# A state-space layer and a dilated attention in one kernel: loads, a matrix's layout and small work moved

## The chip, the cores and the metric

The kernel runs on one core of one Trainium2 chip. The metric is the device time of one execution in microseconds (us), and of several executions the median. The engines are TensorE (PE, matmuls; PEld is its weight loads), VectorE (DVE), ScalarE (ACT), GpSimd (POOL) and SyncE (SP), which issues most of the DMAs.

## The reference

Two layers on two inputs x of 2048 x 448 each, put side by side in the output:

```
A:  Lam_bar = exp(exp(log_dt) * (Lambda_re + i Lambda_im))
    B_bar   = ((Lam_bar - 1) / Lam) * (B_re + i B_im)
    h[t]    = Lam_bar * h[t-1] + B_bar x[t]            (448 complex states, t = 0..2047)
    y[t]    = 2 * Re(C h[t]) + x[t] * Dskip
B:  q, k, v = x @ wqkv  (16 heads of 28)
    logits over the 8 positions s, s-2, ..., s-14; softmax; sum of v; @ wo
```

## The kernel before

**Part B** turns x so that features lie on partitions. The first 512 rows are loaded plainly (`xn`, two DMAs on SP) and turned by PE (`turn_x`, L196, four times four transpositions into PSUM, then a copy by DVE or ACT); the rest comes by transposing DMAs. k's and q's projections (`proj_t`, L253) and v's (`proj`, L239) follow. The logits are products of q with shifted k on DVE (`products`, L298, in six groups of q and k channels, each 1.67 us) summed over channels by PE (`sums`, L315). The softmax (`softmax`, L344) turns the logits back with PE, takes maxima on DVE, subtracts them on PE and exponentiates on ACT. `pv` (L400) is a long line of DVE multiplications and additions; its result is turned by a DMA (`tail`, L422), multiplied by wo on PE (`out`, L432), copied out of PSUM and stored. The last of the four wo steps, `wo[3]`, copies by turns on ACT and DVE (L440).

**Part A** works in real pairs of states, seven blocks m of 64 states, and in time chunks of 16 with four sub-steps b. `params` (L528) computes powers of Lam_bar on DVE and ACT from `prow`, three rows of parameters turned by PE (`turn_params`, L523). `mat` (L596) makes from each power a block matrix on DVE by one broadcast multiplication with `Dm`; B's factor has the key "g" and a layout of its own. Level 1 (`level1_halves`, `level1`) applies B and the powers within a chunk; `scan` (L666) runs seven doubling steps over chunks; `ends` (L689) gives the carried state G; `correct` (L706) adds power times G to each state, either on PE with an identity matmul and a copy by ACT ("A"), or by one matmul and an addition on DVE ("V"); `y` (L722) multiplies by C and adds the skip term by matmuls with `Dg`, four diagonal matrices that `skip` (L580) makes on ACT from `drow`.

**What sets the order.** `lanes` (L97) issues matmuls of half height two at a time, one per half of the array, in numbered steps s; a group must be done on one half before the other half continues it, with a tiny memset on POOL (`spot`) between. `weave` is a list of (step, functions): at that step the functions' work is issued. BEGIN (L46) holds the steps of `first`, `second` and `third`, which start DVE's products and matrices; WEAVE those of the sums; 168 to 211 those of the softmax; 242 that of `skip`. After `lanes`, the remaining level 1, scans, ends and wo steps are issued in program order, and the tail's PE order is written by hand in `line`, with a "V" correction's matmul put in every 1.55 us (L881). `each` (L861) places a correction behind every DVE operation of the last `pv` from the ninth on. `cx.warm` issues matmuls on zeros at the start. Loads on SP run in program order; ACT's queue has three: log_dt's row and the two DMAs of k's weights.

Of the kernel before, what the change touches and what calls it, by code (L numbers as in the profile page):

```python
# [15 lines left out]
bf16 = mybir.dt.bfloat16  # L16

S = 2048
D = 448
T = 16  # L20
NCH = 128
KT = 4
KP = 112
KA = 128
# [10 lines left out]
NM = 7  # L35
MP = 8
PL = 64
# [8 lines left out]
BEGIN = [26, 45, 67]  # L46
# [114 lines left out]
class PartB:  # L161
# [55 lines left out]
    def load_w(self, src, dst, n, eng):  # L217
        v, r = self.B_wqkv[:, src:src + n], (KT - 1) * KA
        eng.dma_start(self.wn[:, 0:KT - 1, dst:dst + n], v[0:r].rearrange("(k p) c -> p k c", p=KA))
        eng.dma_start(self.wn[:, KT - 1, dst:dst + n], v[D - KA:D])  # L220

    def load_wo(self):
        nc = self.nc
        wo = self.wo_p
        wo_v = self.B_wo.rearrange("(h d) c -> h d c", h=H)
        for dl in range(8):
            nc.sync.dma_start(wo[dl * H:(dl + 1) * H, 0, 0:KT - dl // 4], wo_v[:, dl::8])
        nc.sync.dma_start(wo[PL:KA, 1], wo[0:PL, 0])
        nc.sync.dma_start(wo[0:PL, 1, 1:KT], wo[PL:KA, 0, 0:KT - 1])
# [192 lines left out]
    def tail(self, hf, jl0, acc, last):  # L422
        nc, pool, cx = self.nc, self.pool, self.cx
        if self.oT is None:
            self.oT = pool.tile([KA, 2, 14, NCH], bf16, name="oT", tag="bX")
        oT, flat = self.oT[:, self.oi % 2], acc.rearrange("p j d h -> p (j d h)")
        self.oi += 1
        n = 7 if last else 14
        for c in range(0, 14, n):
            nc.sync.dma_start_transpose(oT[:, c:c + n], flat[:, c * KA:(c + n) * KA])  # L430

        def out(i):  # L432
            done = []
            for odd in range(2):
                ps = cx.ps([NCH, D], f32, "wo_ps", "lg")
                for k in range(KT):
                    done.append(nc.tensor.matmul(ps[:], lhsT=oT[:, 7 * i + 3 * odd + k, :], rhs=self.wo_p[:, odd, k, :],  # L437
                                                 start=(k == 0), stop=(k == KT - 1)).ins)
                yb = cx.ya[:, 4 + 2 * i + odd] if last else pool.tile([NCH, D], bf16, name="yb", tag="yb", bufs=4)[:]
                cx.ev("V" if last and odd else "A", yb, ps[:])  # L440
                nc.sync.dma_start(self.out_b[:, hf * HJ + jl0 + 2 * i + odd, :], yb)
            return done

        return out if last else lambda: [out(i) for i in range(2)]


class PartA:
# [25 lines left out]
    def load_params(self):  # L473
        nc, pool = self.nc, self.pool
        self.prow = pool.tile([3 * NM, 2, PL], bf16, name="prow")
        self.drow = pool.tile([KT, KA], bf16, name="drow")
        for i, src in enumerate((self.A_logdt, self.A_Lre, self.A_Lim)):
            v = src.rearrange("(m p) -> m p", p=PL).unsqueeze(1).to_broadcast([NM, 2, PL])
            (nc.scalar, nc.sync, nc.sync)[i].dma_start(self.prow[i * NM:(i + 1) * NM], v)

    def load_d(self):
        nc = self.nc
# [33 lines left out]
    def load_x(self):  # L516
        self.xT = self.pool.tile([KA, 4, KT, NF], bf16, name="xaT", tag="xin")
        xv = self.A_x[0].rearrange("(n b) d -> n b d", b=4)
        for b in range(4):
            self.nc.sync.dma_start_transpose(self.xT[:, b, 0:KT - 1, :], xv[:, b, 0:(KT - 1) * KA])  # L520
            self.nc.sync.dma_start_transpose(self.xT[:, b, KT - 1:KT, :], xv[:, b, D - KA:D])

    def turn_params(self):  # L523
        self.pt = self.cx.ps([NCH, 3 * NM], bf16, "pt_p", "mm")
        self.cx.chain(self.nc.tensor.transpose(self.pt[:], self.prow[:].rearrange("m r p -> m (r p)"),
                                               self.cx.ident[0:3 * NM, 0:3 * NM]).ins)
# [67 lines left out]
            self.cx.order(self.mat(key, self.Scat[:, NPW if i == "g" else i]), after, "NoSync")  # L594

    def mat(self, key, scal):  # L596
        if key == "g":
            sh = [NCH, NM, 2, PL]
            t_ = self.pool.tile(sh, bf16, name="matg")
            in0 = self.Dm[:, :, 0].unsqueeze(1).unsqueeze(1).to_broadcast(sh)  # L600
            in1 = scal[:, :, 0:NM].rearrange("p h m -> p m h").unsqueeze(3).to_broadcast(sh)
            self.mats[key] = t_[:].rearrange("p m h q -> p m (h q)")
        else:
            sh = [NCH, 2, PL, MP]
            t_ = self.pool.tile(sh, bf16, name=f"mat{key}")
            in0, in1 = self.Dm[:].unsqueeze(1).to_broadcast(sh), scal.unsqueeze(2).to_broadcast(sh)
            self.mats[key] = t_[:].rearrange("p h q m -> p m (h q)")
        return self.nc.vector.tensor_tensor(t_[:], in0, in1, op=ALU.mult).ins

    def setup_c(self, *ms):  # L610
# [129 lines left out]
def body(ctx: ExitStack, tc: tile.TileContext, A_x, A_Lre, A_Lim, A_Bre, A_Bim, A_Cre, A_Cim, A_logdt, A_Dskip,  # L740
         B_x, B_wqkv, B_wo, out):
    nc = tc.nc
# [7 lines left out]
    b.alloc()  # L750
    b.load_xn(0, 2)
    a.load_params()
    b.load_w(D, 0, D, nc.scalar)
    b.load_xn(2, 4)
    cx.consts()
    a.consts()
# [11 lines left out]
    b.zero_halo(b.vd)  # L768
    b.load_wo()
    a.load_c()  # L770
    cx.warm(8)
    a.turn_params()
    turns = [lambda i=i: b.turn_x(i, "VAVV"[i], ("pt", "lg")[i // 2]) for i in range(4)]
    for f in turns[:2]:
        for ins in f():
            cx.chain(ins)
    a.params(b.turned["V"])
    cx.warm(2)

# [4 lines left out]
    def early(*keys):  # L784
        for k in keys:
            ins = a.mat("g" if k == "g" else KPOW[k], a.Scat[:, NPW if k == "g" else k])
            if b.product is not None:
                cx.order(ins, b.product, "NoSync")
            b.product = ins

    def first():
        early(0)
        b.products(0, 0)
        return ()

    def second():
        b.products(0, 0, (2,), (2,))
        early(3)
        return ()

    def third():
        b.products(0, 1, (0, 1))
        early("g", 4)
        return ()

    values = [b.proj(j, "A") for j in (*range(HJ, T), 6, 7, 4, 5, 2, 3, 0, 1)]
    qk, soft = b.qk(), {}
    weave = [(5, turns[2:] + [later]), (BEGIN[0], [first]), (BEGIN[1], [second]), (BEGIN[2], [third])]
    weave += [(s_, [f]) for s_, f in zip(WEAVE, qk)]
    weave.sort(key=lambda x: x[0])  # L810

# [24 lines left out]
        return next(soft["pv"]) + next(soft["pv"])  # L836

    weave += [(168, [turn])] + [(171 + 2 * i, [lambda i=i: soft[1][0][2 + i]()]) for i in range(2)] + [(177, [prepare])]
    weave += [(181, [begin]), (199, [more]), (211, [more])]
    weave += [(242, [a.skip])]  # L840
    cx.lanes([b.proj_t(t0, t1, g, "A") for t0, t1, gs in ((0, 256, (0, 1, 2, 4, 5, 6)), (256, 512, (0, 1, 2)), (0, 512, (3,)), (256, 512, (4, 5, 6)))
              for g in gs]
             + [b.proj_t(*t, g, "A") for t in parts for g in range(7)] + values
             + [a.level1_halves(b_, m) for b_ in range(4) for m in range(*MH[0])], weave, 20)
    at0, put, wo = soft[0][1], soft["put"], b.outs
    deque(soft["pv"], 0)
    deque(b.pv(1, soft[1][1], 4, 8, between=[put(11, 12), put(), put(1, 2)]), 0)
    a.alloc_scan()
    for mh in range(3):
        if mh:  # L850
# [5 lines left out]
        a.ends(mh)  # L856
    cx.ya = pool.tile([NCH, 8, D], bf16, name="ya", tag="cn")
    line, extra, steps = [], [], []
    todo = [(b_, m) for b_ in range(3) for m in range(NM)][5:]

    def each(ins):  # L861
        cx.vchain(ins)
        steps.append(ins)
        if len(steps) >= 9 and todo:
            extra.extend(a.correct(*todo.pop(0), "V"))

    def wo_line(lists):
        return [(i, 0.19) for l_ in lists for i in l_]

    for m in range(5):  # L870
        line += a.correct(0, m, "A")
    line += wo_line(wo[1]())
    deque(b.pv(0, at0, 0, 4, each=each), 0)
    deque(b.pv(0, at0, 4, 8, True, each=each), 0)
    for b_, r in itertools.product((3, 0, 1, 2), range(4)):
        line += a.y(r, b_)
# [41 lines left out]
```

## Time and profile before

| what | us |
|---|---|
| median of 3 runs (143.95, 144.22, 144.97) | 144.22 |
| the profiled execution | 144.79 |
| its span, first to last instruction | 142.7 |
| PE busy | 135.9 |
| DVE busy | 125.5 |
| ACT busy | 88.0 |
| PE's first matmul at | 1.25 |
| DVE's last pv operation ends at | 132.10 |

The profile is one execution. Times in it are from the span's start. A row of the timeline gives start, duration, engine, line, operation and shapes, and in brackets how long the engine had been idle and what ended that. Rows of several instructions in a pipeline last longer than their number times the distance of two: three matrices take 1.89 us, so 0.61 each, where one alone takes 0.67 to 0.69.

### The profile page before, as it was taken

The page shows a single profiled execution, that of the slowest core. Times are in us where ns is not written, and L with a number is a line of the kernel's source. Part 1 is how long each engine was busy: PE and PEld are TensorE (multiplying, and loading weights), DVE is VectorE, ACT ScalarE, POOL GpSimd, SP SyncE. Part 2 cuts the span into 40 slices and gives each one's busy share as a digit, 9 for nine tenths or more (in the row PEclk, how much of TensorE's full clock was granted, in tenths as well). Part 3 has the DMA queues.
Part 4 walks back from the last instruction along what each step waited for, and adds up shares of the span by engine and source line. Part 5 has one row for each costly group of instructions (what it writes and reads, how often), then busy time and mean ns, then how long its engine had stood idle before and what let it go on. Part 6 is the DMA issues. An engine that isn't in the chain of part 4 may idle for free.

```text
span 142.7 us, 3299 instructions
## 1 busy us (share of the span) xinstructions
PE 135.9 (95%) x1259; PEld 77.9 (55%) x1263; DVE 125.5 (88%) x157; ACT 88.0 (62%) x193; POOL 10.6 (7%) x108
## 2 busy tenths in 40 slices
PE   6999999999999999999969999999999999999991
PEld 2466445444566654356645655569555655555540
DVE  4499989989999889999999999999799999999011
ACT  3476678667686653845599976899862322345440
POOL 7311100101010001001120000000000000000000
PEclk9999999999999999999999999999999999999999
DMA  4979899999964869990042000082012731112963
GB/s 107 303 155 158 185 228 114 195 194 158 176 117 97 179 102 259 253 218 8 0 82 47 5 0 0 10 183 71 0 67 96 158 103 64 64 64 96 138 214 103
DMA packets 45166, 17.03 MB, mean 119 GB/s; under 512 B 37267, under 2 KB 44769, under 8 KB 45151
## 3 DMA queue, kind: packets, MB, share of 16 engines
q1 hardware_dynamic: 44586, 16.36, 55.9%
q10 hardware_dynamic: 565, 0.46, 1.1%
q8 instruction: 10, 0.16, 0.6%
q14 instruction: 5, 0.04, 0.1%
HBM read 3.91 MB, written 3.67 MB: 53 GB/s over the span
## 4 chain that ended last, share of the span: by engine, by line
PE 78%; DVE 9%; ACT 9%; issue 2%; POOL 0%; ACTq 0%; DVEq 0%; POOLq 0%
PE qk_ps L130 16%; PE y_ps L731 15%; PE l1h L130 7%; PE l L639 7%; PE wo_ps L437 6%; PE v_ps L130 5%; PE lg L323 5%; PE co L711 3%; PE warm L73 3%; ACT G L703 2%; DVE pr L312 2%; PE y_ps L727 2%; PE l L684 2%; ACT pbuf L687 2%; DVE pvb L414 1%
## 5 line engine op out<-in xcount | busy, mean ns | idle before, releaser
L414 DVE TENSOR_TENSOR pvb<-attn,vd 128x1792 bf16<-128x1792 bf16 (+1 forms) x33 | 34.3, 1055 | 0.0
L417 DVE TENSOR_TENSOR pvb<-pvb 128x1792 bf16<-128x1792 bf16 (+1 forms) x29 | 30.5, 1051 | 0.3
L130 PE MATMUL qk_ps<-xbT,wqkv_nat 64*128 64x512 bf16 (+1 forms) x210 | 24.0, 335 | 0.4 <-POOL spot L139 0.3
L312 DVE TENSOR_TENSOR pr<-q,kd 128x3072 bf16<-128x3072 bf16 x11 | 19.0, 1753 | 1.0 <-ACT q L156 0.6
L734 ACT CAST ya<-y_ps 128x448 bf16<-128x448 f32 x16 | 8.5, 532 | 18.5 <-PE y_ps L731 18.5
L731 PE MATMUL y_ps<-Ccat,h 128*128 128x448 bf16 x84 | 18.7, 352 | 0.0
L130 PEld LDWEIGHTS <-wqkv_nat 64*128 64x128 bf16 x210 | 11.0, 94 | 10.8 <-POOL spot L139 3.1
L130 PE MATMUL l1h<-xaT,Bcat 64*128 64x512 bf16 x112 | 15.6, 377 | 0.0
L437 PE MATMUL wo_ps<-wo_p,oT 128*128 128x448 bf16 x64 | 14.1, 352 | 0.0
L156 ACT CAST kd<-qk_ps 128x512 bf16<-128x512 f32 (+4 forms) x26 | 10.4, 423 | 4.5 <-PE qk_ps L130 4.3
L130 PE MATMUL v_ps<-wqkv_nat,xbT 64*128 64x448 bf16 x112 | 13.1, 361 | 0.0
L639 PE MATMUL l<-xaT,Bcat 128*128 128x512 bf16 x45 | 12.6, 379 | 0.1
L715 DVE TENSOR_TENSOR h<-co,h 128x512 bf16<-128x512 f32 x16 | 10.9, 683 | 0.8 <-PE co L711 0.7
L156 ACT CAST q<-qk_ps 128x512 bf16<-128x512 f32 (+2 forms) x23 | 9.9, 455 | 2.0 <-PE qk_ps L130 1.9
L731 PEld LDWEIGHTS <-h 128*128 128x128 bf16 x84 | 7.6, 98 | 5.6
L130 PEld LDWEIGHTS <-Bcat 64*128 64x128 bf16 x112 | 7.1, 94 | 5.5 <-issue 0.8
L139 POOL MEMSET spot<- 1x1 f32 x63 | 5.6, 89 | 59.3 <-PE qk_ps L130 25.8
L156 ACT CAST vd<-v_ps 128x448 bf16<-128x448 f32 x16 | 7.6, 528 | 3.7 <-PE v_ps L130 3.5
L650 ACT CAST h<-l1h 128x512 bf16<-128x512 f32 x12 | 6.4, 592 | 5.7 <-PE l1h L130 5.7
L130 PEld LDWEIGHTS <-xbT 64*128 64x128 bf16 x112 | 7.3, 145 | 4.1 <-issue 1.3
L687 ACT CAST pbuf<-l 128x512 bf16<-128x512 f32 (+2 forms) x21 | 8.9, 425 | 1.0 <-PE l L684 0.8
L312 DVE TENSOR_TENSOR kd<-q,kd 128x3072 bf16<-128x3072 bf16 x5 | 8.8, 1755 | 0.7 <-ACT q L156 0.7
(133 smaller groups left out, 212.7 us busy)
## 6 DMA issues: line engine op xcount, KB each, us to landing
out_dram<-ya SPq DMA_DIRECT2D x20, 112.0 KB, 1.7
out_dram<-yb SPq DMA_DIRECT2D x12, 112.0 KB, 1.8
vd<-vd SPq DMA_DIRECT2D x1, 784.0 KB, 5.4
wqkv_nat<-in_B_wqkv_dram SPq DMA_DIRECT2D x2, 336.0 KB
vd<-vd SPq DMA_DIRECT2D x1, 588.0 KB
xn<-in_B_x_dram SPq DMA_DIRECT2D x2, 224.0 KB, 3.9
cn<-in_A_C_re_dram SPq DMA_DIRECT2D x4, 98.0 KB, 3.2
cn<-in_A_C_im_dram SPq DMA_DIRECT2D x4, 98.0 KB, 3.4
```

Source lines behind the costliest of these rows:

```text
L130: ins = mm(g["ps"], lhsT=l_, rhs=r_, start=first, stop=not (g["left"][0] or g["left"][1]), skip_group_check=True).ins
L156: return self.nc.scalar.copy(out, in_).ins
L312: self.queued(V.tensor_tensor(pr, q[0][:, qu].unsqueeze(2).to_broadcast([KA, KT - 1, 4, n]), self.shifted(self.kT[:, 2 * i + qu], s), op=A ...
L323: out.append(mm(lg[32 * t:32 * t + 32, n * qu:n * qu + n], lhsT=l_, rhs=r_, start=not (s or qu or c), stop=(s == 1 and c == KT - 1), skip_ ...
L414: each(V.tensor_tensor(t_[:, c0:c1], at[:, w, jl0 + c0:jl0 + c1, :].unsqueeze(2).to_broadcast([NCH, c1 - c0, DH, H]), self.vd[:, off + c0: ...
L417: ins = V.tensor_tensor(acc[:, c0:c1], acc[:, c0:c1], t_[:, c0:c1], op=ALU.add).ins
L437: done.append(nc.tensor.matmul(ps[:], lhsT=oT[:, 7 * i + 3 * odd + k, :], rhs=self.wo_p[:, odd, k, :], start=(k == 0), stop=(k == KT - 1)) ...
L639: nc.tensor.matmul(ps[:], lhsT=self.Bcat[:, m, k, :], rhs=self.xT[:, b, k, :], start=(k == 0), stop=(b == 0 and k == KT - 1))
L687: nc.scalar.copy(dst[:, :, PAD:], ps[:])
L715: cx.vchain(nc.vector.tensor_tensor(h, ps[:], h, op=ALU.add).ins)
L731: out.append(nc.tensor.matmul(ps[:], lhsT=self.state(m, r, b), rhs=self.C[:, m, :], start=False, stop=(m == NM - 1), skip_group_check=True ...
L734: nc.scalar.copy(ya, ps[:])
```

## The change

- k's weights: four row blocks in two DMAs, blocks 0 and 1 on SP, 2 and 3 on ACT's queue, where it was blocks 0 to 2 and then 3, both on ACT's. Lambda_im's row goes to ACT's queue, ahead of the weights; SP issues its half of the weights in that row's place, ahead of the second half of x.
- Seven warm-up matmuls instead of eight at the start; the first turn of x precedes the turn of the parameters; the third and fourth turn of x come at step 8 instead of 5.
- B's factor matrix is made in the layout of the other matrices (one form for all).
- DVE's order: matrix 1 comes after the third step's edge products, matrix 4 between the two next products, and the two last scan matrices right after "g" and 8, where they were made in the second `pv`.
- The softmax's `more` of step 199 comes at 201; `skip` at 206 instead of 242.
- Three corrections by ACT instead of five, eighteen by DVE instead of sixteen, beginning one `pv` operation later.
- The last `wo` step: three copies by ACT, the fourth halved between ACT and DVE.

```diff
+    def load_wk(self):
+
+        v = self.B_wqkv[:, D:2 * D]
+        self.nc.sync.dma_start(self.wn[:, 0:2, 0:D], v[0:2 * KA].rearrange("(k p) c -> p k c", p=KA))
+        v = v[2 * KA:3 * KA].unsqueeze(1)
+        v = bass.AP(v.tensor, v.offset, [list(v.ap[0]), [v.ap[0][0] * (D - 3 * KA), 2], list(v.ap[2])])
+        self.nc.scalar.dma_start(self.wn[:, 2:KT, 0:D], v)
...
-                cx.ev("V" if last and odd else "A", yb, ps[:])
+                half = D // 2 if last and i and odd else D
+                cx.ev("A", yb[:, 0:half], ps[:, 0:half])
+                if half < D:
+                    cx.ev("V", yb[:, half:], ps[:, half:])
...
-            (nc.scalar, nc.sync, nc.sync)[i].dma_start(self.prow[i * NM:(i + 1) * NM], v)
+            (nc.scalar, nc.sync, nc.scalar)[i].dma_start(self.prow[i * NM:(i + 1) * NM], v)
...
+    pt = None
+
     def turn_params(self):
+        if self.pt is not None:
+            return
...
     def mat(self, key, scal):
-        if key == "g":
-            sh = [NCH, NM, 2, PL]
-            t_ = self.pool.tile(sh, bf16, name="matg")
-            in0 = self.Dm[:, :, 0].unsqueeze(1).unsqueeze(1).to_broadcast(sh)
-            in1 = scal[:, :, 0:NM].rearrange("p h m -> p m h").unsqueeze(3).to_broadcast(sh)
-            self.mats[key] = t_[:].rearrange("p m h q -> p m (h q)")
-        else:
-            sh = [NCH, 2, PL, MP]
...
+        sh = [NCH, 2, PL, MP]
+        t_ = self.pool.tile(sh, bf16, name=f"mat{key}")
+        in0, in1 = self.Dm[:].unsqueeze(1).to_broadcast(sh), scal.unsqueeze(2).to_broadcast(sh)
+        self.mats[key] = t_[:].rearrange("p h q m -> p m (h q)")
...
-    b.load_w(D, 0, D, nc.scalar)
+    b.load_wk()
...
-    cx.warm(8)
-    a.turn_params()
+    cx.warm(7)
...
     for f in turns[:2]:
         for ins in f():
             cx.chain(ins)
+        a.turn_params()
...
     def first():
-        early(0)
         b.products(0, 0)
...
     def second():
         b.products(0, 0, (2,), (2,))
-        early(3)
+        early(0)
...
     def third():
-        b.products(0, 1, (0, 1))
-        early("g", 4)
+        b.products(0, 1, (0,))
+        early(3)
+        b.products(0, 1, (1,))
+        early("g", 4, 11, 12)
...
-    weave = [(5, turns[2:] + [later]), (BEGIN[0], [first]), (BEGIN[1], [second]), (BEGIN[2], [third])]
+    weave = [(8, turns[2:] + [later]), (BEGIN[0], [first]), (BEGIN[1], [second]), (BEGIN[2], [third])]
...
-    weave += [(181, [begin]), (199, [more]), (211, [more])]
-    weave += [(242, [a.skip])]
+    weave += [(181, [begin]), (201, [more]), (211, [more])]
+    weave += [(206, [a.skip])]
...
-    deque(b.pv(1, soft[1][1], 4, 8, between=[put(11, 12), put(), put(1, 2)]), 0)
+    deque(b.pv(1, soft[1][1], 4, 8, between=[put(), put(), put(1, 2)]), 0)
...
-    todo = [(b_, m) for b_ in range(3) for m in range(NM)][5:]
+    todo = [(b_, m) for b_ in range(3) for m in range(NM)][3:]
...
-        if len(steps) >= 9 and todo:
+        if len(steps) >= 10 and todo:
...
-    for m in range(5):
+    for m in range(3):
         line += a.correct(0, m, "A")
```

In the built program, PE has three matmuls fewer, DVE the same products and pv operations in the same order, and SP and ACT's queue as many DMAs as before; the lanes' own order of matmuls is unchanged but for what is woven in. On SP one store of `wo[2]` now stands ahead of the first of the last two transpositions instead of behind it.

More of the change, by code (lines that the diff above doesn't have):

```diff
@@ L596, in mat @@
     def mat(self, key, scal):
-        if key == "g":
-            sh = [NCH, NM, 2, PL]
-            t_ = self.pool.tile(sh, bf16, name="matg")
-            in0 = self.Dm[:, :, 0].unsqueeze(1).unsqueeze(1).to_broadcast(sh)
-            in1 = scal[:, :, 0:NM].rearrange("p h m -> p m h").unsqueeze(3).to_broadcast(sh)
-            self.mats[key] = t_[:].rearrange("p m h q -> p m (h q)")
-        else:
-            sh = [NCH, 2, PL, MP]
-            t_ = self.pool.tile(sh, bf16, name=f"mat{key}")
-            in0, in1 = self.Dm[:].unsqueeze(1).to_broadcast(sh), scal.unsqueeze(2).to_broadcast(sh)
-            self.mats[key] = t_[:].rearrange("p h q m -> p m (h q)")
+        sh = [NCH, 2, PL, MP]
+        t_ = self.pool.tile(sh, bf16, name=f"mat{key}")
+        in0, in1 = self.Dm[:].unsqueeze(1).to_broadcast(sh), scal.unsqueeze(2).to_broadcast(sh)
+        self.mats[key] = t_[:].rearrange("p h q m -> p m (h q)")
         return self.nc.vector.tensor_tensor(t_[:], in0, in1, op=ALU.mult).ins
@@ L838, in body @@
     weave += [(168, [turn])] + [(171 + 2 * i, [lambda i=i: soft[1][0][2 + i]()]) for i in range(2)] + [(177, [prepare])]
-    weave += [(181, [begin]), (199, [more]), (211, [more])]
-    weave += [(242, [a.skip])]
+    weave += [(181, [begin]), (201, [more]), (211, [more])]
+    weave += [(206, [a.skip])]
+    weave.sort(key=lambda x: x[0])
     cx.lanes([b.proj_t(t0, t1, g, "A") for t0, t1, gs in ((0, 256, (0, 1, 2, 4, 5, 6)), (256, 512, (0, 1, 2)), (0, 512, (3,)), (256, 512, (4, 5, 6)))
```

## The prediction

> **What bounds the kernel now.** I read the busy shares, then the chain that ended last, then the timelines of TensorE (PE), VectorE (DVE) and ScalarE (ACT) at each gap that the chain shows, then the landings of the first transfers.
>
> ```profile
> PE 135.9 (95%) x1259; PEld 77.9 (55%) x1263; DVE 125.5 (88%) x157; ACT 88.0 (62%) x193; POOL 10.6 (7%) x108
> PE 78%; DVE 9%; ACT 9%; issue 2%; POOL 0%; ACTq 0%; DVEq 0%; POOLq 0%
> ```
>
> PE is idle for 6.8 us of the span in all: 1.25 before its first matmul and about 3.1 after its last, so some 2.4 between. A gain has to come out of those, or out of matmuls removed.
>
> ```profile
> 1.25 3.60 PE warm L73 x8
> 4.84 0.13 PE pt_p L525
> 4.97 0.96 PE pt_x L201 x8
> 5.94 0.85 PE warm L73 x2
> 6.79 0.65 PE qk_ps L130 x8
> 7.44 0.55 PE pt_x L201 x8
> 70.17 0.17 ACT dsk L585
> 70.42 1.28 ACT Dg L588 x4
> 136.40 3.16 PE wo_ps L437 x16
> 139.58 0.62 DVE ya L158
> ```
>
> These are rows of the chain. At the start ten warm-up matmuls, the parameters' transposition and x's stand ahead of the first projection. At 70 us ACT makes the skip matrices (1.44 us) ahead of level 1's last copies. The end is PE work without a gap, then one DVE eviction.
>
> ```profile
> 59.56 0.38 PE L362 MATMUL lt<-mx,nident 128*128 128x512 bf16 x1 [0.24 <-DVE mx L357]
> 72.70 0.22 PE L674 MATMUL l<-h,ident 128*128 128x128 bf16 x1 [0.95 <-ACT h L652]
> 61.80 1.07 ACT L650 CAST h<-l1h 128x512 bf16<-128x512 f32 x2 [1.23 <-PE l1h L130]
> 20.70 1.75 DVE L608 TENSOR_TENSOR matg<-Dm,Scat 128x896 bf16<-128x896 bf16 x1
> 22.38 0.67 DVE L608 TENSOR_TENSOR mat<-Dm,Scat 128x1024 bf16<-128x1024 bf16 x1
> 23.36 1.76 DVE L312 TENSOR_TENSOR pr<-q,kd 128x3072 bf16<-128x3072 bf16 x1 [0.32 <-ACT q L156]
> 100.56 0.69 DVE L715 TENSOR_TENSOR h<-co,h 128x512 bf16<-128x512 f32 x1 [0.67 <-PE co L711]
> ```
>
> Timeline rows: start, time, then in brackets the idle time before. PE waits 0.24 us for the maxima and 0.95 us for ACT's copies; DVE is full, with short waits.
>
> **The change part by part.** Minus is a gain.
>
> *Start.* The first half of x lands at 0.80 + 2.8 = 3.60 us (the shortest landing of `xn`), yet its transposition begins at 4.97, behind eight warm-ups and the parameters. With seven warm-ups (0.427 each) PE is free at 1.25 + 7 x 0.427 = 4.24. Eight transpositions and `pt_p`, 1.09, end at 5.33 instead of 5.93; ACT's copy of the second half then ends 0.79 before or at the first projection as now (5.93 to 6.72), which comes at 6.1 to 6.2 instead of 6.72. What could take this away is late data: the third and fourth rows of k's weights land at 1.86 + 4.7 = 6.56 and the second half of x at 2.07 + 4.9 = 6.97, and its transposition began at 7.37. Weave point 8 instead of 5 puts six more projection matmuls (3 steps of 0.11 = 0.33) ahead of that transposition. I take -0.35, near that 0.33, which holds even if x's second half lands no earlier. Bounds: -0.6 (all of the 0.6 by which the transpositions end earlier) and +0.3 (k's first rows, now third on SP, as late as today's 6.56 plus the 0.4 that passed between 6.97 and 7.37: 6.96 against 6.72). Log_dt and Lambda_im share ACT's queue ahead of the weights; SP keeps its number of transfers.
>
> The Trainium skill ("DMA: Bandwidth & Descriptors", Issuing engines are not separate DMA queues) says that transfers from any engine run on the same 16 DMA engines, so a second queue saves only issue time. By that the weights' last rows would still land near 6.56, the first projection would stay at 6.72 and the sum below would be 1.84 instead of 2.19. The row that bears on it is the landing of 4.7 us on ACT's queue against 3.3 for the transfer just ahead of it.
>
> The Trainium skill ("TensorE: Matmul & The Clock Gate", The HAM clock gate) says that full clock comes after a window of about 3.4 us of activity, whatever the number of matmuls. The trace agrees that the clock doubled: eight transpositions took 0.96 us at 4.97 and 0.55 at 7.44. By the rule the projections reached early would still run at half speed, as priced in rival 2 (sum 1.93).
>
> *VectorE's order up to 53 us.* B's factor matrix in the others' layout takes 0.67 instead of 1.75 (pipelined 0.61 instead of 1.68): -1.07. Matrix 1 moves from before the first product (where DVE waited 0.31 anyway) to behind the third step's edge products, in matrix 4's place; matrix 4 moves to the wait of 0.41 before the product at 19.02. The two last scan matrices come in from the later pv stage (+1.2). From 19.2 on: product to 20.87, then four matrices of 0.61 to 23.3, where the next product waits until 23.36 for q. So nothing is late and this costs 0. If the cover is gone (q earlier than DVE), it costs at most 0.6 + 1.2 - 1.07 = 0.73 of DVE time, less the 0.43 that DVE waits for q at 31.76; the sums of products on PE are then late by up to 0.3. Bounds 0 and +0.3.
>
> *Maxima, two steps later* (201 for 199). PE's 0.24 wait at 59.56 is filled by four level-1 matmuls (0.43). -0.24, bounds -0.24 and 0.
>
> *Skip row at 206.* (a) ACT's 1.44 us leaves the place before level 1's last copies. Those of m = 1 and 0 can start when their sums are done (70.4 and 70.7), those of 3 and 2 at 71.6 and 72.15; they ended at 72.13, 72.66, 73.14 and 73.63, and end at 71.03, 71.56, 72.15, 72.68. The scan starts when PE is free (71.75 instead of 72.70) and gets its last block at 72.73 instead of 73.67: -0.94. Later waits in 73 to 97 are ACT's and PE's own chain, which moves as a whole, so I keep all of it; bounds -1.3 (ACT's 1.44 less the tiny transposition) and 0 (the ACT chain of 89 to 97 eats it). (b) Where it goes, ACT idled 1.23 us before 61.80. `pt_d` comes at about 61.15, the skip matrices end near 62.9, so the next copies of h start 1.05 late and end at 64.95 instead of 64.66. The matmul that reads the last of them stands at 64.90, now 64.78: a stall of about 0.25 with the semaphore. +0.25, bounds 0 and +0.5. Queued behind the moved work on ACT are those four copies alone.
>
> *Two corrections from ACT to DVE.* PE loses two identity matmuls: 2 x 0.216 = -0.43. Also the first correction that DVE takes needs G of block 3 instead of 5, so the wait for ACT's G before 100.09 goes: -0.12 (PE's last G matmul began at 99.75 with 0.22), bounds 0 and -0.3. DVE gets 2 x 0.60 more here and 1.2 fewer matrices before; it arrives at its first correction at 99.89 - 1.2 + 1.0 (one pv operation more ahead of it) = 99.7, while PE offers it at about 99.4, so the wait of 0.67 goes and DVE ends at 131.4 instead of 132.10 (both less the start's gain). Corrections come every 1.61 us on DVE and 1.555 on PE; the 18th ends at 99.7 + 17 x 1.61 + 0.7 = 127.8, before PE's y of that block at about 129.1. No wait there.
>
> *End.* SP's last transposition was issued at 132.92 and landed 3.8 us later, 136.72, now 136.05; PE's last eight matmuls begin at 136.24 + 8 x 0.19 = 137.76, less the 0.94, 0.12 and 0.43 gained before them 136.3 (all less the start's gain). Cover 0.25 us. The third of the last four evictions no longer waits for DVE (0.62 against ACT's 0.53): -0.09. The last one is cut between ACT and DVE: a 256-wide ACT copy takes 0.37, so about 0.35 instead of 0.62: -0.27, bounds 0 (if the two serialize on one PSUM tile) and -0.35. One store moves ahead of a transposition on SP (0.53 us, its data ready 1 us before): 0.
>
> **Sum:** -0.35 - 0 - 0.24 - 0.94 + 0.25 - 0.12 - 0.43 - 0.09 - 0.27 = -2.19. The profiled execution took 144.79 (span 142.7, 2.1 around it), 0.57 above the median of 144.22; it would become 142.6, the median 142.0.
>
> **Rivals.**
> 1. *DVE sets the end.* If the moved matrices are not covered, DVE ends 0.73 later, the last transposition lands at 136.8 instead of 136.05 and PE waits 0.5: 142.5. For it: the cover is 0.25. Against: q was waited for at 23.36 and 31.76.
> 2. *The start gives nothing*, since weights and x land as before (6.56, 6.97): 142.4; at the bad bound of +0.3, 142.7. Or PE is still at half speed from 6.2 to 6.72 (the transpositions at 4.97 are, the matmuls from 6.79 are not): half of 0.52 is given back, 142.3. For it: the same bytes wait in the same order of landing; PE's speed was not raised by x's data.
> 3. *ACT's chain takes the skip row's gain back*: ACT is busy 11.2 of 12 us in 88 to 100 and the chain of waits runs on it there: 142.0 + 0.94 = 143.0. Against: that chain starts from the scan, which moves.
> 4. *Slower: the parameters block x.* `pt_p` now stands between x's two transpositions on PE and needs all three parameter rows, one now behind log_dt on ACT's queue. Every microsecond that it lands late stops x's second half, and all after it. The gain is eaten when `pt_p` starts 2.2 late, at 7.0, that is with a landing near 6.6, which the last transfer of ACT's queue had (6.56). Against: it is 1.8 KB and second in that queue.
>
> **How the numbers follow.** Chances: forecast 0.60, rival 1 0.12, rival 2 0.12, rival 3 0.11, rival 4 0.05. Predicted 142.0. The likeliest case alone spans 141.4 to 142.6; with rivals 1 to 3 and the better bounds of skip row and start (0.36 and 0.25 more) 141.2 to 143.3. A measurement here tells about 1% (1.44 us) from no change. Below 142.78 lie nearly all of the forecast, most of rivals 1 and 2 and little of 3: 0.74; within 1%: 0.21; slower: 0.05.
>
> **What would show it.** Start right: first projection near 6.2, x's transposition at 4.3. Skip row right: scan's first matmul right after level 1 with no wait for ACT, a small gap near 64.8. VectorE right: matg near 0.67, the product after four matrices still waits for q. Tail right: no wait for G, DVE's end near 131, PE not idle before its last eight matmuls. Wrong if PE waits before `pt_p`, if the scan starts earlier but y does not, or if PE idles for the last transposition.

## The result and the profile after

| | before | after |
|---|---|---|
| median, us | 144.43 (143.95 to 144.97) | 142.69 (142.56 to 142.93) |
| ratio of the times | | 0.988, 95% interval 0.984 to 0.992 |
| the profiled execution, us | 144.79 | 142.57 |
| its span, us | 142.7 | 140.5 |

The change saves 1.74 us by the medians and 2.22 in the two profiled executions. The forecast was 142.0 with a range of 141.2 to 143.3. The page of the profile after, busy shares and the shares of the chain that ended last:

```profile
PE 134.3 (96%) x1260; PEld 76.9 (55%) x1260; DVE 124.4 (89%) x158; ACT 88.0 (63%) x193; POOL 10.6 (8%) x108
PE 79%; DMA 6%; ACT 6%; DVE 4%; issue 1%; SPq 1%; POOL 0%; ACTq 0%; POOLq 0%
```

PE is busy 1.6 us less, DVE's and ACT's shares in the chain went from 9% each to 4% and 6%, and a new one has come: DMA, 6%. The chain of waits of the same kernel, in order of time (start, length, what), shows where:

```profile
1.75 4.30 DMA wqkv_nat<-in_B_wqkv_dram
...
129.15 4.74 DMA oT<-pvb
133.94 3.24 PE wo_ps L445 x16
137.20 0.35 ACT ya L156
137.57 0.39 DVE ya L158
```

The first projection waits for k's weights, the last 16 wo matmuls for the last transposition but one, and the two halves of the last eviction stand one behind the other. The timeline of the same kernel (start, length, engine, line, operation; in brackets the idle time before and what ended it):

```profile
4.85 0.59 PE L73 MATMUL warm<-wz 128*128 128x512 bf16 x2
6.10 1.21 PE L130 MATMUL qk_ps<-xbT,wqkv_nat 64*128 64x256 bf16 x14 [0.66 <-DMA wqkv_nat<-in_B_wqkv_dram]
20.21 0.69 DVE L616 TENSOR_TENSOR matg<-Dm,Scat 128x1024 bf16<-128x1024 bf16 x1
...
31.17 1.76 DVE L320 TENSOR_TENSOR kd<-q,kd 128x3072 bf16<-128x3072 bf16 x1 [0.42 <-ACT q L156]
...
58.78 0.61 PE L370 MATMUL lt<-mx,nident 128*128 128x512 bf16 x2
...
70.85 0.23 PE L682 MATMUL l<-h,ident 128*128 128x128 bf16 x1
99.01 0.68 DVE L723 TENSOR_TENSOR h<-co,h 128x512 bf16<-128x512 f32 x1
129.65 0.62 DVE L425 TENSOR_TENSOR pvb<-pvb 128x896 bf16<-128x896 bf16 x1
132.30 1.49 PE L739 MATMUL y_ps<-Ccat,h 128*128 128x448 bf16 x7
133.93 2.79 PEld L445 LDWEIGHTS <-oT 128*128 128x128 bf16 x16 [0.59 <-DMA oT<-pvb]
137.57 0.39 DVE L158 CAST ya<-wo_ps 128x224 bf16<-128x224 f32 x1 [7.30 <-ACT ya L156]
```

The waits for the maxima (0.24), for ACT's copies before the scan (0.95) and for the first correction (0.67) have no bracket any more, and `matg` takes 0.69. New is the bracket of 0.59 at the weight load (PEld) of wo. PEld runs ahead of PE, so its 0.59 is not what PE lost: the last seven y matmuls begin at 132.30 and take 0.19 each, so the next matmul was due at 133.63 and came at 133.94, 0.31 late. The last row says that DVE's half of the last eviction was released by ACT's half.

### The profile page after: what moved, and what is told of

Same layout as the page of the kernel before. It is cut to its first block, busy times and chain, and to the rows that moved or that the text cites. A ratio compares the mean times of both kernels' runs of the same rounds, so it can differ in the third digit from the quotient of the medians.

```text
span 140.5 us, 3301 instructions
## 1 busy us (share of the span) xinstructions
PE 134.3 (96%) x1260; PEld 76.9 (55%) x1260; DVE 124.4 (89%) x158; ACT 88.0 (63%) x193; POOL 10.6 (8%) x108
## 4 chain that ended last, share of the span: by engine, by line
PE 79%; DMA 6%; ACT 6%; DVE 4%; issue 1%; SPq 1%; POOL 0%; ACTq 0%; POOLq 0%
PE qk_ps L130 17%; PE y_ps L739 12%; PE l1h L130 10%; PE l L647 7%; PE wo_ps L445 7%; PE v_ps L130 6%; PE lg L331 5%; DMA oT<-pvb 3%; PE co L719 3%; DMA wqkv_nat<-in_B_wqkv_dram 3%; DVE pr L320 2%; PE gt L709 2%; PE l L692 2%; PE y_ps L735 2%; ACT h L660 2%; ACT pbuf L695 2%
## 5 line engine op out<-in xcount | busy, mean ns | idle before, releaser
L647 PE MATMUL l<-xaT,Bcat 128*128 128x512 bf16 x48 | 13.1, 379 | 0.0
L723 DVE TENSOR_TENSOR h<-co,h 128x512 bf16<-128x512 f32 x18 | 12.3, 681 | 0.0
L445 PEld LDWEIGHTS <-oT 128*128 128x128 bf16 x64 | 5.9, 97 | 5.6 <-DMA oT<-pvb 0.6
```

Of the source, the lines that this page charges most:

```text
L647: nc.tensor.matmul(ps[:], lhsT=self.Bcat[:, m, k, :], rhs=self.xT[:, b, k, :], start=(k == 0), stop=(b == 0 and k == KT - 1))
L723: cx.vchain(nc.vector.tensor_tensor(h, ps[:], h, op=ALU.add).ins)
```

## The experiments

Most of these kernels are the changed kernel with one edit. The first is the changed kernel without any, "early matrix, two PSUM tiles" joins two edits and "nineteen corrections" three; two are the kernel before with one part of the change alone. Medians, and the ratio to the kernel before on the same chip:

| kernel | median, us | before | ratio (95%) |
|---|---|---|---|
| changed kernel, again | 142.72 | 144.56 | 0.988 (0.986 to 0.990) |
| skip row at 242 again | 143.30 | 144.38 | 0.991 (0.989 to 0.994) |
| old start | 143.03 | 144.38 | 0.989 (0.986 to 0.992) |
| five corrections by ACT | 143.59 | 144.38 | 0.993 (0.991 to 0.996) |
| matrix 1 early | 142.46 | 144.38 | 0.986 (0.983 to 0.989) |
| before + new start | 144.41 | 144.56 | 0.999 (0.997 to 1.001) |
| last eviction whole | 142.77 | 144.56 | 0.988 (0.985 to 0.990) |
| early matrix, two PSUM tiles | 142.29 | 144.56 | 0.985 (0.983 to 0.988) |
| before + skip row at 206 | 143.25 | 144.48 | 0.993 (0.990 to 0.995) |
| old layout of "g" | 143.39 | 144.48 | 0.993 (0.991 to 0.996) |
| fetch earlier | 142.46 | 144.48 | 0.987 (0.984 to 0.989) |
| nineteen corrections | 142.41 | 144.48 | 0.986 (0.983 to 0.989) |

Differences of 0.2 to 0.6 us are near what the medians tell apart, so each profile is read too, "at an equal start": its times less the amount by which DVE's first product comes later than 10.71, where it comes in the changed kernel's profile. Why this is needed is the first finding.

**The start: the whole of it undone, and it alone.**

```diff
-    b.load_wk()
+    b.load_w(D, 0, D, nc.scalar)
...
-            (nc.scalar, nc.sync, nc.scalar)[i].dma_start(self.prow[i * NM:(i + 1) * NM], v)
+            (nc.scalar, nc.sync, nc.sync)[i].dma_start(self.prow[i * NM:(i + 1) * NM], v)
...
-    cx.warm(7)
+    cx.warm(8)
+    a.turn_params()
...
-    weave = [(8, turns[2:] + [later]), (BEGIN[0], [first]), (BEGIN[1], [second]), (BEGIN[2], [third])]
+    weave = [(5, turns[2:] + [later]), (BEGIN[0], [first]), (BEGIN[1], [second]), (BEGIN[2], [third])]
```

> The changed kernel with the whole start undone: k's weights in two DMAs on ACT's queue, Lambda_im on SP, eight warm-ups and the parameters' transposition ahead of x's, x's second half at step 5. Theory: the first projection comes at about 6.7 instead of 6.10, the first product on DVE 0.57 later than 10.71, and all of it, PE and DVE alike, runs 0.57 later to the end: 143.26. Rival (the 0.57 came from the phase of TensorE's clock in the one profiled execution, full speed from 4.14 us instead of 6.74): medians differ by less than 0.2 us, 142.7 to 142.9, and the profile's start depends on when the clock rises.

The start's rows in the timeline of this kernel, and then of the kernel before:

```profile
4.77 0.62 PE L201 MATMUL pt_x<-ident,xn 128*128 128x128 bf16 x8
5.22 0.59 PE L73 MATMUL warm<-wz 128*128 128x512 bf16 x2
6.06 0.84 PE L130 MATMUL qk_ps<-xbT,wqkv_nat 64*128 64x256 bf16 x8 [0.24 <-DVE karg L562]
```

```profile
4.90 1.03 PE L201 MATMUL pt_x<-ident,xn 128*128 128x128 bf16 x8
5.73 1.06 PE L73 MATMUL warm<-wz 128*128 128x512 bf16 x2
```

The same instructions, and the same order of loads: eight transpositions take 0.62 here and 1.03 there, two warm-ups 0.59 and 1.06. The clock differs. The trace records when TensorE is granted full clock: at 4.22 us in this execution, at 6.74 in the profile before, and at 4.14 in the profile after. The old start thus reached the first projection at 6.06, as early as the new one (6.10). The expected 0.57 fell as an effect of the start: most of it was the clock. The median of this kernel, 143.03, lies between the two expectations, 0.34 above the changed kernel's 142.69; by the ratios to the kernel before, which was timed beside each, it is 0.14 to 0.17.

> The kernel before, with the whole new start and nothing else of the change. Theory (phase of the clock): of the 0.57 us by which the changed kernel's profile started earlier, most is that the clock rose at 4.14 us there and at 6.74 in the profile before; at a like rise the two starts differ by 0.04 (4.14 against 4.22) to 0.1 (6.91 against 6.74). The median is 0 to 0.2 us under that of the kernel before, and the profile's first product follows the clock's rise as above. Rival (the gain is the start's own): 0.5 to 0.6 under it.

> The changed kernel itself once more, as the measure for the kernels beside it. In six profiles so far the clock that TensorE is granted rises to full between 4.14 and 6.91 us after the span's start, whatever the kernel, and the first product on VectorE comes at 10.71 to 11.20 with the changed start. Expected: median 142.6 to 142.9; its profile's first product is near 10.7 if the clock rises before 5, near 10.86 if between 5 and 6.2, near 11.2 if near 7; the wait for the last transposition but one is there again if one sixteenth of that DMA lands 1.6 us behind the others again.

The new start alone gives a ratio of 0.999, that is -0.15 us (-0.39 to +0.10). So both ways give about 0.15, and neither tells it from nothing or from 0.35. All profiles, by when the clock rose:

| kernel (start) | full clock from | first product on DVE |
|---|---|---|
| changed (new) | 4.14 | 10.71 |
| old start (old) | 4.22 | 10.75 |
| changed, again (new) | 4.98 | 10.86 |
| nineteen (new) | 5.00 | 10.62 |
| skip at 242, old "g", matrix early, two tiles (new) | 5.29 to 5.85 | 10.86 |
| before + skip row (old) | 6.00 | 11.15 |
| fetch earlier (new) | 6.05 | 10.95 |
| before (old) | 6.74 | 11.28 |
| five corrections (new) | 6.91 | 11.20 |
| last whole (new) | 7.18 | 11.23 |
| before + new start (new) | 4.83 | 11.40 |

At a like clock the new start is ahead by 0.04 (4.14 against 4.22), 0.20 (6.05 against 6.00) and 0.08 (6.91 against 6.74). The clock does not settle it alone: the changed kernel, again, with the rise at 4.98, came to 10.86 where 10.7 was expected. The last row is the other limit; the timeline of that kernel:

```profile
6.78 1.21 PE L130 MATMUL qk_ps<-xbT,wqkv_nat 64*128 64x256 bf16 x14 [1.06 <-DMA wqkv_nat<-in_B_wqkv_dram]
```

PE had ended its warm-ups at 5.72 and waited 1.06 us, since the last sixteenth of k's first rows landed at 6.74, 1.15 after the median one. The new start brings k's first rows later: their DMA was complete at 5.52 to 6.74 in the eleven profiles with the new start and at 4.71 to 5.84 in the three with the old one. So the new start waits for the weights (0.66 us in the changed kernel) where the old one, in the profile before, went from the warm-ups at half clock straight into the projection. As far as these profiles show, it gains where the clock rises late, and loses that again where the weights land late. The Trainium skill ("TensorE: Matmul & The Clock Gate", What's actually happening) gives a free-running window of 3.4 us as the reason for such a spread; the rises here lie between 4.14 and 7.18, 3.0 apart, whatever the kernel, which agrees with one such window, though the page speaks of 500 ns either way; the measured spread is the larger one. At an equal start, the changed kernel's last copy ends at 137.96 and that of the kernel before at 140.20 - 0.57 = 139.63: 1.67 saved. With the start's 0.15 this is 1.82, beside 1.74 and 1.84 by the medians of two comparisons.

**The skip row: undone, and alone.**

```diff
-    weave += [(206, [a.skip])]
+    weave += [(242, [a.skip])]
```

> The changed kernel (median 142.69, profiled 142.57) with the skip row's work back at step 242. Theory: the four skip matrices stand again ahead of level 1's last copies, PE waits about 0.95 us for ACT before the scan's first matmul (70.85 becomes about 71.8), and the last y starts about 0.9 later than 132.30. But the changed kernel idles 0.59 us on PE for the last transposition but one, which hangs on DVE and not on the scan; a later PE uses that up first. So the end moves by only 0.95 - 0.59 = 0.36 to 0.6 us: 143.0 to 143.3, and the wait at the last wo step is gone. Rival (ACT's chain of 89 to 97 us had eaten the gain): the scan is later but the first correction is not, and the end does not move: 142.7. Second rival (the whole term reaches the end): +0.95, 143.6.

> The kernel before, with the skip row's work at step 206 and nothing else of the change. Theory: the wait of 0.95 us for ACT before the scan's first matmul goes, four copies of h start about 1 us later where PE has at most 0.05 to lose, and the whole gain reaches the end, since here the transpositions at the end have 2 us of cover: -0.9 to -1.05 against the kernel before, 143.5. Rival (ACT's chain of 89 to 97 us takes it back): scan earlier, first correction not, 0 to -0.2. Second rival (part is given back at the copies of h, as predicted 0.25): -0.7.

Timeline of the changed kernel with the skip row at 242, and then of the kernel before with the skip row at 206:

```profile
71.93 0.22 PE L682 MATMUL l<-h,ident 128*128 128x128 bf16 x1 [0.95 <-ACT h L660]
...
133.37 1.49 PE L739 MATMUL y_ps<-Ccat,h 128*128 128x448 bf16 x7
134.69 3.21 PE L445 MATMUL wo_ps<-wo_p,oT 128*128 128x448 bf16 x16
```

```profile
71.65 0.23 PE L674 MATMUL l<-h,ident 128*128 128x128 bf16 x1
...
133.87 1.49 PE L731 MATMUL y_ps<-Ccat,h 128*128 128x448 bf16 x7
```

At an equal start (0.15) the scan is 0.93 later and the last y 0.92, but the last wo matmuls only 0.60, and so is the end (median +0.61): y runs straight into wo, with no wait for the transposition. The 0.31 that a later PE does not feel is that wait. Alone in the kernel before, where the transpositions have cover, the step gives all of it: last y 133.87 against 134.91, less 0.13 of start, -0.91; end -0.90; median -1.05 (-0.66 to -1.45). So ACT's chain of 89 to 97 us takes nothing back. The four copies that the step delays cost 0.06, not 0.25: from the maxima to the last copies of level 1 (the 37th to the 133rd of its 136 matmuls, by their starts) it is 12.42 us with the skip row at 206 and 12.36 at 242 in the kernel before, 12.07 and 12.01 in the changed one.

**The maxima, from the same profiles.** No kernel undoes this step alone, but three of the fourteen have `more` at 199 (before, before + new start, before + skip row) and eleven at 201. The two matmuls that wait for the maxima began 0.63 us apart before and do so 0.23 apart in the changed kernel; the first of them, before:

```profile
58.93 0.39 PE L362 MATMUL lt<-mx,nident 128*128 128x512 bf16 x1
```

Level 1's first part has the same 136 matmuls in all fourteen. From the start of its 37th to that of its 49th, a stretch in which these two lie, 2.34 us pass in each of the three and 1.98 or 1.99 in each of the eleven. The step so gained 0.36, more than the wait of 0.24 that the bracket showed.

**B's factor matrix in its old layout.**

```diff
+        if key == "g":
+            sh = [NCH, NM, 2, PL]
...
```

> The changed kernel with B's factor matrix in its old layout. Theory (the cover is used up to the last tenth): the matrix takes 1.75 us instead of 0.69, the next product starts at about 23.9 instead of 22.8, the wait of 0.42 for q at 31.17 takes part of the 1.07 back, and 0.3 to 0.65 stays in TensorE's sums of products and in VectorE's line to its first correction. At the end it is partly hidden again, since the changed kernel idles 0.31 on PE for the last transposition but one: 142.8 to 143.3. Rival (hidden altogether, sums have cover of their own): product late, scan and end not, 142.7.

Timeline, DVE, of this kernel:

```profile
20.37 1.76 DVE L623 TENSOR_TENSOR matg<-Dm,Scat 128x896 bf16<-128x896 bf16 x1
...
23.84 1.75 DVE L320 TENSOR_TENSOR pr<-q,kd 128x3072 bf16<-128x3072 bf16 x1
...
31.94 1.76 DVE L320 TENSOR_TENSOR kd<-q,kd 128x3072 bf16<-128x3072 bf16 x1
```

The wait of 0.42 at 31.17 is gone, and the product there is 31.94 - 0.15 - 31.17 = 0.62 late. All of that reaches the end (+0.61 in the profile, +0.70 in the median), near 1.07 - 0.42 = 0.65; the expectation had part of it hidden at the end, and none was: the last wo matmuls waited for the transposition here too. Four matrices in a row cost nothing only because one of them got shorter.

**Corrections: five by ACT again, and one more by DVE.**

```diff
-    todo = [(b_, m) for b_ in range(3) for m in range(NM)][3:]
+    todo = [(b_, m) for b_ in range(3) for m in range(NM)][5:]
...
-        if len(steps) >= 10 and todo:
+        if len(steps) >= 9 and todo:
...
-    for m in range(3):
+    for m in range(5):
```

> The changed kernel with five corrections by ACT and sixteen by DVE from the ninth pv operation on, as before the change. Theory: PE has two identity matmuls more (+0.43) and DVE's first correction waits for two more G blocks (about +0.2), so PE reaches the last wo step at 133.35 + 0.6 = 133.95 to 134.05; DVE has two corrections less and ends about 1.2 earlier, so the last transposition but one is in time and the wait of 0.59 goes. The end moves by 0 to 0.2 us: 142.7 to 142.9, where the sum of the prediction says 0.43 + 0.12 = 0.55 or, as measured, 0.70. Rival: both terms reach the end in full, 143.2 to 143.4.

The expectation missed. At an equal start (0.49) the last y is 0.78 later (G wait 0.27, identity matmuls and the rest 0.51) and the wo wait is gone, so the end is +0.46. I had taken PEld's 0.59 for PE's loss, which is 0.31. The median is +0.90; the 0.4 beyond the profile's reading is not settled. Nor did two corrections less (1.2 us) bring DVE's end forward: 130.74 - 0.49 = 130.25, as in the changed kernel (130.27). The wait of 0.62 for the first correction's matmul, which needs G, is back, and more sums follow their products directly. DVE's timeline in this kernel:

```profile
96.39 1.08 DVE L422 TENSOR_TENSOR pvb<-attn,vd 128x1792 bf16<-128x1792 bf16 x1
97.50 1.09 DVE L425 TENSOR_TENSOR pvb<-pvb 128x1792 bf16<-128x1792 bf16 x1
99.22 0.69 DVE L723 TENSOR_TENSOR h<-co,h 128x512 bf16<-128x512 f32 x1 [0.62 <-PE co L719]
...
103.22 1.08 DVE L422 TENSOR_TENSOR pvb<-attn,vd 128x1792 bf16<-128x1792 bf16 x1
104.22 0.68 DVE L723 TENSOR_TENSOR h<-co,h 128x512 bf16<-128x512 f32 x1
```

A sum that stands right behind its own product starts 1.11 after it (96.39, 97.50); with a correction between, the product holds the engine for 1.00. A correction put in there so costs 0.60 - 0.11 = 0.49 net.

```diff
-    todo = [(b_, m) for b_ in range(3) for m in range(NM)][3:]
+    todo = [(b_, m) for b_ in range(3) for m in range(NM)][2:]
...
-    for m in range(3):
+    for m in range(2):
```

> The version with matrix 1 ahead of the first product and the last wo matmuls in two PSUM tiles (142.29), and one correction more by VectorE: nineteen, two by ACT. Theory (the corrections' balance is used up): PE loses one identity matmul and the wait for one block of G, -0.22 - 0.13, but VectorE's line is 0.60 longer and the last transposition lands that much later, where it had 0.2 us of cover: PE waits 0.6 + 0.35 - 0.2 = 0.75 before its last eight matmuls, net +0.4: 142.7. Rival (the last transposition is bound by SP's queue or has more cover): -0.35, 141.9.

Its timeline:

```profile
131.94 1.49 PE L739 MATMUL y_ps<-Ccat,h 128*128 128x448 bf16 x7
133.96 3.23 PE L448 MATMUL wo_ps<-wo_p,oT 128*128 128x448 bf16 x20 [0.53 <-DMA oT<-pvb]
```

This one starts from the version of the last experiment below (142.29), and the diff shows only what is new in it. It comes to 142.41; no gain, but not by the mechanism that I named. The last y came 0.26 earlier than in that version at an equal start, and PE then lost 0.69 (133.96 instead of 131.94 + 7 x 0.19 = 133.27) to the last transposition but one, not the last: all sixteen parts of it landed 4.7 us after its issue. Why the whole transfer was late is not settled; on these runs nineteen bring nothing over eighteen.

**Matrix 1 ahead of the first product.**

```diff
     def first():
+        early(0)
...
     def second():
...
-        early(0)
+        early(1)
...
-    deque(b.pv(1, soft[1][1], 4, 8, between=[put(), put(), put(1, 2)]), 0)
+    deque(b.pv(1, soft[1][1], 4, 8, between=[put(), put(), put(2)]), 0)
```

> The changed kernel with matrix 1 made ahead of the first product, where DVE idles 0.69 us, matrix 2 in its place behind the third step's edge products, and so only one matrix left in the second pv. Theory (DVE's line, through the last transposition but one, now sets the end): DVE is 0.6 us shorter behind 60 us, its last pv operation ends near 129.7 instead of 130.27, the transposition is issued 0.6 earlier and PE no longer idles 0.59 at the last wo step: -0.3 to -0.59, 142.1 to 142.4. Rival (the wait comes from one late sixteenth of the transposition's DMA and not from DVE): it lands as late as before, no change, 142.7. Second rival (the matrix at the start delays the first product by its 0.69): sums and all behind it up to 0.3 later, 142.9.

Timeline:

```profile
10.86 1.76 DVE L320 TENSOR_TENSOR pr<-q,kd 128x3072 bf16<-128x3072 bf16 x1 [0.34 <-ACT q L156]
...
132.44 1.49 PE L739 MATMUL y_ps<-Ccat,h 128*128 128x448 bf16 x7
133.77 3.21 PE L445 MATMUL wo_ps<-wo_p,oT 128*128 128x448 bf16 x16
```

The matrix fits into DVE's idle time (0.34 of it is left), the first product is where others with that clock have it, the wait is gone, and the end is 0.32 earlier at an equal start; median 142.46. DVE ended 0.43 earlier, but the transposition gained more: it landed at 131.75, its last part within 0.14 of the first, where in the changed kernel fifteen parts were there by 132.3 and the last at 133.89. So this run does not separate DVE's line from the late sixteenth. The next does.

**The late sixteenth.**

```diff
     cx.warm(2)
+    wp = cx.ps([NCH, 4 * NCH], f32, "warm", "lg")
+    for i in range(6):
+        cx.chain(nc.tensor.matmul(wp[:, 0:16], lhsT=cx.wz[:, 0:NCH], rhs=cx.wz[:, 0:16], start=True, stop=True).ins)
```

> The changed kernel with six matmuls of 16 columns on zeros more, behind the two warm-ups at the start, where PE waits for k's weights anyhow: twelve PE instructions of no work. In the changed kernel a 16 KB instruction fetch starts on the DMA 0.3 us before the last transposition but one lands, and one sixteenth of that lands 1.6 us behind the rest; PE then loses 0.31 (133.94 instead of 133.63). Fetches come every 256 PE instructions or so, so twelve more move the fetch about 1.2 us earlier against the work. Theory (the fetch holds the sixteenth back): all sixteen parts land within 0.2 us, no wait, -0.3: 142.4. Rival (something else holds it): the sixteenth is late as before, 142.7. Second rival: it holds back another part of the same transfer, 142.6 to 142.7.

Timeline:

```profile
132.50 1.49 PE L739 MATMUL y_ps<-Ccat,h 128*128 128x448 bf16 x7
133.83 3.21 PE L445 MATMUL wo_ps<-wo_p,oT 128*128 128x448 bf16 x16
```

DVE's work is as in the changed kernel, and the transposition is issued at the same time at an equal start. The 16 KB fetch came at 130.45 instead of 131.88, all sixteen parts landed between 132.98 and 133.12, PE did not wait, and the end is 0.35 earlier at an equal start (142.46). So twelve PE instructions without work took the wait away, with DVE's end where it was: DVE's line had cover (fifteen parts were there by 132.32, and PE needed them at 133.63). In the five profiles with a late part (the changed kernel twice, old start, last whole, old "g") the fetch began 0.30 or 0.31 before the first part landed and took 0.95 us; in the seven without one where the fetch lay near it, 0.36 to 0.39 before, and took 1.17 to 1.52. Counted from the issue of the transposition, the fetch began 2.37 to 2.39 us behind it in these seven and 2.61 to 2.75 in those five. With nineteen corrections, where all parts were late, it was 2.73 and again 0.95 us long. That fetch and transfer meet on one DMA engine fits this; the trace does not name the engine, so it is not shown. Nor is it why the first part came 0.6 later here than in the changed kernel.

**The last eviction: whole, and out of two PSUM tiles.**

```diff
-                half = D // 2 if last and i and odd else D
+                half = D
```

> The changed kernel with the very last eviction whole on ACT, not cut. Theory (the two halves run one after the other, 0.35 and 0.39 with a gap, since they read one PSUM tile): the last copy ends 0.53 us after its start at PE's end instead of 0.76, -0.23: 142.4 to 142.5 against the changed kernel's 142.6 to 142.7. Rival (the halves overlap in effect, or the store behind them hides it): no change.

Its last copy in the timeline:

```profile
137.77 0.53 ACT L156 CAST ya<-wo_ps 128x448 bf16<-128x448 f32 x1 [0.23 <-PE wo_ps L445]
```

The end is 0.18 earlier at an equal start (138.30 - 0.52 against 137.96). The medians (142.77 and 142.72) do not show it; the five runs of this kernel lie between 142.32 and 142.93, too far apart for 0.18.

The next kernel has the edit of "matrix 1 ahead of the first product" as well; the diff shows what is new:

```diff
+                for c0 in range(0, D, half):
+                    ps = cx.ps([NCH, half], f32, "wo_ps", "pt" if c0 else "lg")
...
+                    cx.ev("V" if c0 else "A", yb[:, c0:c0 + half], ps[:])
```

> The changed kernel with matrix 1 ahead of the first product and matrix 2 in its place (as measured alone: 142.46, the wait at the last wo step gone, -0.31 at an equal start), and the last wo matmuls cut into two PSUM tiles of 224 columns: ACT copies the first while PE makes the second, which DVE copies. Theory: the copy of the first half is hidden and the end comes 0.43 after PE's last matmul instead of 0.80, less 0 to 0.1 for four matmuls more: -0.31 - 0.3 = 142.0 to 142.1. Rival (shorter matmuls cost as much as long ones, or the copies still wait for each other): 142.4.

Timeline:

```profile
133.77 3.22 PE L448 MATMUL wo_ps<-wo_p,oT 128*128 128x448 bf16 x20
136.26 0.78 ACT L156 CAST ya<-wo_ps 128x448 bf16<-128x448 f32 x2 [0.25 <-PE wo_ps L448]
137.03 0.39 DVE L158 CAST ya<-wo_ps 128x224 bf16<-128x224 f32 x1 [7.03 <-DMA out_dram<-ya]
```

Twenty matmuls, the last eight half as wide, take the time of sixteen; ACT's half copy lies beside them, and DVE ends at 137.42, 0.43 after PE, as expected. With the early matrix this is the lowest median, 142.29 (142.07 to 142.53, where the changed kernel, again, had 142.62 to 142.79). Against the changed kernel the medians give -0.43, the profiles at an equal start -0.69; 142.0 to 142.1 was expected. The Trainium skill ("PSUM — Partial Sum Buffer", PSUM bank collisions raise a hardware error) forbids two engines in one PSUM bank at once, so the halves of one tile must wait for each other; the rows agree: 0.35 and then 0.39 out of one tile, and ACT's half side by side with PE out of two.

## Why the prediction was right, and where it was not

The direction, the size of the largest term and the range held; the point was 0.7 too low, and 142.69 lies just above the 142.6 at which the likeliest case alone was to end. Of the 0.7, 0.2 to 0.3 is the base: the three runs shown had a median of 144.22, with the result it was 144.43, and later comparisons had 144.38 to 144.56. Term by term ("after" means the profile after, at an equal start):

| term | predicted | measured |
|---|---|---|
| start | -0.35 | -0.15 (before + new start; interval -0.39 to +0.10); -0.57 in the two profiles |
| VectorE's order | 0 | 0; +0.61 with the old layout |
| maxima | -0.24 | -0.36 (the same stretch of level 1, 2.34 and 1.98; not tried alone) |
| skip row, (a) + (b) | -0.94 + 0.25 | -0.90 alone |
| wait for G | -0.12 | -0.27 |
| two identity matmuls | -0.43 | -0.50 |
| third-last eviction | -0.09 | -0.09 |
| last transposition but one | 0 (cover) | +0.31 |
| last eviction cut | -0.27 | +0.14 |

The measured rows without the start add up to -1.67, which is what was saved at an equal start. That the sum came this near is partly luck: maxima, skip row, G and identity matmuls gave 0.55 more than forecast, the end 0.72 less, and the start by its own median 0.20 less.

- **Start.** The weak step is "I take -0.35, near that 0.33, which holds even if x's second half lands no earlier". It looked for the bound at x; in the profiles the first projection waits for the weights (0.66 and 1.06 us). The prediction took the third and fourth rows of k's weights to land at 6.56 before; only the fourth did, and the first three had landed at 4.71. The change so moved the first two from 4.71 to 6.05, which it counted only in its bad bound. The row that I read PE's 0.96 for eight transpositions from was one phase of the clock. The size stays open: the interval holds -0.35 as well as nothing. Rival 2 (142.4) named the right term, though not its reason: the data did not land as before.
- **Maxima.** Right in kind, mis-sized: 0.24 was the bracketed wait alone and was also put as the better bound; 0.36 was gained.
- **Skip row.** (a) was right: from the last matmuls of level 1 to the scan it is 0.98 shorter. (b) was near its low bound: 0.06 in place of 0.25. Rival 3 fell: alone, the gain reaches the end.
- **VectorE's order.** Right. The old layout bears out the argument, that the cover is used up; the moved matrices were not undone by themselves.
- **Wait for G and corrections.** Right in kind; the wait for G was sized at half its worth.
- **End.** Two steps failed. "Cover 0.25 us" was worked out for the last transposition; the one before it had 1.3 us of cover by its first fifteen parts (132.32, needed at 133.63) and lost it to the sixteenth (133.89). Rival 1 named a wait of PE for a transposition, with DVE's end as its cause; DVE ended earlier than forecast (130.27; the forecast was 131.4 less the start's gain), and "fetch earlier" has no wait at the same end of DVE. "-0.27, bounds 0 (if the two serialize on one PSUM tile)" named the right doubt and took the other side; the bound of 0 was also too good, since two copies behind each other, 0.76 with the gap, are longer than the one of 0.62 that they replace. Out of two PSUM tiles they are not.
- **Rival 4** did not occur: `pt_p` started at 4.50, right behind four of x's transpositions.

## What to carry to other kernels

Before a saving at the start is read from two profiles, compare the clock of both: the first product of one and the same start came between 10.71 and 11.23 in kernels that differ only behind it, more than the edit was to bring. Where two engines are both near full, undo one edit and also make it alone: the skip row was worth 0.90 alone and 0.60 in the finished kernel, where 0.31 of it had gone into the wait for a transposition. A last eviction that is cut in two paid here only with a PSUM tile for each half.

## What the runs showed of the hardware that was not expected

- Full clock on TensorE came between 4.14 and 7.18 us after the span's start, with the first matmul at 1.25 in all fourteen profiles.
- One sixteenth of a transposing DMA landed 1.6 us behind the other fifteen in five of fourteen profiles; at the start the last sixteenth of k's first rows landed 1.15 behind the median one.
- On DVE, a sum directly behind the product that it reads started 1.11 us after it; with another instruction between, the product held the engine for 1.00.
- Two matmuls of 224 columns took no longer than one of 448 (twelve whole and eight halves in 3.22 us, sixteen whole in 3.21).
